# Two-sequence 64x64 products, a first inverse done whole on VectorE, eight steps scored ahead, and one idle product per step in a delta-rule attention kernel with a mixture of experts

## The chip, the cores and the metric

The kernel runs on one core of a Trainium2 chip. The metric is the device time of one execution in microseconds (us), over runs of the same program. One more execution was recorded by the hardware profiler; all durations below come from that one. PE is TensorE (matmuls), PEld its weight loads, DVE is VectorE, ACT is ScalarE, POOL is GpSimd, SP is the engine that issues most transfers. L12 is line 12 of the kernel before.

## The reference

Attention with the delta rule over 4 sequences, 8 heads, 768 tokens, head size 48; its output is reshaped to 3072 tokens of 384 and goes through 8 experts, one per token.

```python
k_n = k / (np.linalg.norm(k, axis=-1, keepdims=True) + 1e-06)
for t in range(S):
    kt, vt, bt = (k_n[:, :, t], v[:, :, t], beta[:, :, t, None])
    y[:, :, t] = np.einsum('bhd,bhde->bhe', q[:, :, t], state)
    v_old = np.einsum('bhde,bhd->bhe', state, kt)
    state = state + bt[:, :, :, None] * np.einsum('bhd,bhe->bhde', kt, vt - v_old)
...
expert_idx = np.argmax(x @ w_gate, axis=1)
h = np.maximum(x_sorted[lo:hi] @ w1[e], 0.0)
y_sorted[lo:hi] = h @ w2[e]
return (gate_w[:, None] * y).astype(np.float32)
```

## The kernel before

The 768 tokens are cut into 24 blocks of 32, one per **step** of the loop at L697. The 128 partitions hold 4 sequences of 32 tokens. Four consecutive steps are a **group**; there are 6 groups. A block is solved with the inverse of a 32x32 triangular matrix per sequence and head, so that a step needs only a few products:

- `by_state` (L453) multiplies keys with the state and gives `R` on top of an identity product of the scaled values (L439); ACT copies it out (L464).
- `logits` (L558, and every fourth step L605 for the ranks) is the router's share for the step before. The instructions in L473 come after ACT has copied the logits (L562).
- The **block product** L473 multiplies the inverse `ub` with `R`: 8 heads times 4 sequences in 32x32 tiles, one per sequence. ACT copies the result to `Z` (L479).
- `by_state` again for the queries (L453 into `pq`), then the state's update (L492), which ACT copies to `states` in two halves (L500).
- The outputs of the step before are turned (L538, copied by L543), then the **masked product** L511 multiplies the masked query-key scores `qk` with `Z`, again 32 products in 32x32 tiles, and ACT copies it to `xg` (L521).
- `score` (L230 in the first `FRONT` = 6 steps, L242 later) makes the key-key and query-key products of a later step. `keep_scores` (L260) masks both on DVE. When a group has its fourth score, `invert` is put on the list `behind`.

The order is written out by hand: each engine works strictly through its own list, in the order of the calls. The inverse is a Python generator; `fill(us)` sends its instructions to DVE in portions, priced with a built-in estimate, 4.0 after each step's products and 2.8 before its `keep_scores`. At the first step of a group, whatever is left of that group's inverse is sent first (L699). When two inverses are on the list, `fill` alternates between them.

The first group's inverse is built in a short form: two 16x16 halves at once on DVE (`K` = 2), and the corner by two products per step on PE (`across`, L384 and L398, with an addition on DVE, L406). These run as `chore`s inside steps 0 to 3. Later groups are inverted whole: 30 pairs of a product (L350) and an addition (L355).

After six scores PE runs ten idle products of 128x512 (`heat`, L431), and one in each step that has nothing left to score. Steps 0, 5 and 8 score one extra step (`EXTRA`). The loads of a step's keys and queries are issued `LEAD` + 2 = 12 steps ahead on SP's queue.

After the loop come the rest of the routing, 24 idle products, and the experts (L775 on), which the change does not touch.

Of the kernel before, what the change touches and what calls it, by code (L numbers as in the profile page):

```python
# [13 lines left out]
FP32 = mybir.dt.float32  # L14
# [26 lines left out]
FRONT = 6  # L41
EXTRA = (0, 5, 8)
LG = DM
RK = LG + E
LEAD = 10
# [4 lines left out]
def _f32_consts():  # L50

    p = np.arange(128)[:, None]
    j = np.arange(128)[None, :]
    rev = np.broadcast_to(E - np.arange(E), (128, E))
    base = np.broadcast_to(np.arange(E) * LIST, (128, E))
    more = np.arange(E)[:, None] * LIST + CAP + np.arange(MAXR)[None, :] * 128  # L60
    more = np.broadcast_to(more.reshape(1, -1), (128, E * MAXR))
    t, w = p % C, j[:, :C]
    own = t // (C // 2) == w // (C // 2)
    kk = 1.0 * (t == w) - (t < w)
    k0 = 1.0 * (t == w) - ((t < w) & own) - (t // (C // 2) > w // (C // 2))
    return np.concatenate(
        [kk, k0, -1.0 * (t < w), rev, base, more, p < j, np.ones((128, 128))], axis=1
    ).astype(np.float32)
# [3 lines left out]
def kernel(  # L72
# [23 lines left out]
    nc.scalar.dma_start(out=cf[:, 0 : 3 * C], in_=src[:, 0 : 3 * C])  # L96
# [4 lines left out]
    def part(w):  # L101
# [4 lines left out]
    mask_g, mask_0, mask_q, rev, base, further, upper, ones = (  # L106
        part(w) for w in (C, C, C, E, E, E * MAXR, 128, 128)
# [51 lines left out]
    warm = persist.tile([128, 512], FP32, name="warm")  # L159
    fdt = persist.tile([128, GS * H, C], FP32, name="fdt")  # L160
# [5 lines left out]
    behind, later, soon, chores = deque(), deque(), deque(), deque()  # L166
    scored, front = [0], [None]
# [3 lines left out]

    def fill(us):


        while us > 0 and behind:
            n = next(behind[0], None)
            if n is None:
                behind.popleft()
                continue
            us -= (0.09 if len(behind) > 1 else 0.165) + 0.00104 * n  # L180
            if len(behind) > 1:
                behind[0], behind[1] = behind[1], behind[0]

    def chore():
        if chores:
            chores.popleft()()
# [62 lines left out]
    def keep_scores(c, pa):  # L249
        if pa is None:  # L250
            return
        g, s = divmod(c, GS)
        if s == 0:
            gts[g] = block.tile([128, GS * H, C], FP32, name="gt", bufs=3)
        qks[c] = stage.tile([128, H, C], FP32, name="qk", bufs=LEAD + 2)
        for out, part, mask in (
            (gts[g][:, H * s : H * s + H, :], pa[:, :, :, 0], mask_g if g else mask_0),
            (qks[c][:], pa[:, :, :, 1], mask_q),
        ):
            nc.vector.tensor_tensor(  # L260
                out=out.rearrange("q (p e) w -> q p e w", e=2), in0=part,
                in1=mask.unsqueeze(1).unsqueeze(1).to_broadcast([128, NP, 2, C]), op=OP.mult,
            )
        if s == GS - 1:
            behind.append(invert(g))

    def invert(g):

        gt = gts[g]
        K = 1 if g else 2
        W = C // K
        ut = block.tile([128, C * C + C], FP32, name="ut")
        full = ut[:, 0 : C * C].rearrange("p (j i) -> p j i", i=C)
        ud = ut[:].rearrange("p (k n) -> p k n", k=K)[:, :, 0 : W * C].rearrange(
            "p k (j i) -> p k j i", i=C
        )
# [12 lines left out]
        if K > 1:  # L291
            nc.vector.memset(full[:, 0:W, W:C], 0.0)
# [38 lines left out]
        w2 = wt[:].rearrange("p (k i) -> p k i", k=K)  # L331

        parts = [(0, W, W)] if K > 1 else [(0, W // 2, W // 2), (W // 2, W, W)]

        def scaled(by_row):
            for a, b, n in parts:
                v = ud[:, :, a:b, 0:n]
                w = w2[:, :, 0:n].unsqueeze(2) if by_row else w2[:, :, a:b].unsqueeze(3)
                nc.vector.tensor_tensor(
                    out=v, in0=v, in1=w.to_broadcast([128, K, b - a, n]), op=OP.mult  # L340
                )
                yield K * (b - a) * n
# [3 lines left out]
        for j in range(W - 2, 0, -1):  # L346
            n = W - 1 - j
            tmp = block.tile([128, C * C // 4], FP32, name="tmp", bufs=4)
            tv = tmp[:, 0 : K * j * n].rearrange("p (k w i) -> p k w i", k=K, i=j)
            nc.vector.tensor_tensor(  # L350
                out=tv, in0=ud[:, :, j + 1 : W, j].unsqueeze(3).to_broadcast([128, K, n, j]),
                in1=ud[:, :, j, 0:j].unsqueeze(2).to_broadcast([128, K, n, j]), op=OP.mult,
            )
            yield K * j * n
            nc.vector.tensor_tensor(  # L355
                out=ud[:, :, j + 1 : W, 0:j], in0=ud[:, :, j + 1 : W, 0:j], in1=tv, op=OP.add
            )
            yield K * j * n
        yield from scaled(False)
        ub = block.tile([128, GS * H, C], FP32, name="ub", bufs=3)  # L360
# [5 lines left out]
        if K > 1:  # L366
            nc.vector.transpose(
                out=fdt[:, :, 0:W].rearrange("p s i -> p i s"),
                in_=full[:, :, 0:W].rearrange("p j i -> p i j"),
            )  # L370
            yield 1024
            for s in range(GS):
                chores.append(partial(across, g, s))
        ubs[g] = ub

    def across(g, s):

        gt, ub = gts[g], ubs[g]
        W = C // 2
        po = front[0][:, 1, DM:512]  # L380
        for h in range(H):
            sh = H * s + h
            for b in range(B):
                nc.tensor.matmul(  # L384
                    po[rows_of(b), W * h : W * h + W], lhsT=gt[rows_of(b), sh, :],
                    rhs=ub[rows_of(b), sh, W:C], start=True, stop=True, skip_group_check=True,
                )
        m1 = work.tile([128, H, W], FP32, name="m1")
        nc.scalar.activation(
            out=m1[:].rearrange("p h w -> p (h w)"), in_=po, func=AF.Copy  # L390
        )

        def second():
            po = front[0][:, 1, DM:512]
            for h in range(H):
                sh = H * s + h
                for b in range(B):
                    nc.tensor.matmul(  # L398
                        po[rows_of(b), W * h : W * h + W], lhsT=fdt[rows_of(b), sh, :],
                        rhs=m1[rows_of(b), h, :], start=True, stop=True, skip_group_check=True,  # L400
                    )
            chores.appendleft(partial(added, po))

        def added(po):
            part = ub[:, H * s : H * s + H, W:C]
            nc.vector.tensor_tensor(  # L406
                out=part, in0=part, in1=po.rearrange("p (h w) -> p h w", h=H), op=OP.add
            )

        chores.appendleft(second)  # L410
# [16 lines left out]
    def heat(n=1):  # L427

        pa = psA.tile([128, 512], FP32, name="pa", tag="pa")
        for _ in range(n):  # L430
            nc.tensor.matmul(  # L431
                pa[:], lhsT=ident[:], rhs=warm[:], start=True, stop=True, skip_group_check=True
            )
# [11 lines left out]
    def step(c):  # L445
# [13 lines left out]
        if c == 0:  # L459
            R = vs  # L460
        else:
            by_state(pc[:, 0, :], 0, False)
            R = work.tile([128, H, D], FP32, name="R")
            nc.scalar.activation(  # L464
                out=R[:].rearrange("q h w -> q (h w)"), in_=pc[:, 0, 0:DM], func=AF.Copy
            )
            logits()
        scale_v(c + 1, 0)
        if c == NS - 1:
            turn(c - 1, psA.tile([128, 512], FP32, name="pa", tag="pa"))  # L470
        for h in range(H):
            for b in range(B):
                nc.tensor.matmul(  # L473
                    pc[rows_of(b), 1, D * h : D * h + D], lhsT=ub[rows_of(b), H * s + h, :],
                    rhs=R[rows_of(b), h, :], start=(h == 0), stop=True, skip_group_check=True,
                )
        chore()
# [10 lines left out]
        if c < NS - 1:  # L488
# [17 lines left out]
            chore()  # L506
        else:
            logits()
        for h in range(H):
            for b in range(B):  # L510
                nc.tensor.matmul(  # L511
                    pq[rows_of(b), D * h : D * h + D], lhsT=qk[rows_of(b), h, :],
                    rhs=Z[rows_of(b), h, :],
# [8 lines left out]
        nc.sync.dma_start(out=xs[128 * c : 128 * c + 128, 0:DM], in_=x)  # L522
        return extra
# [145 lines left out]
    nc.gpsimd.memset(warm[:], 0.0)  # L669
    nc.gpsimd.memset(fdt[:], 0.0)  # L670
    nc.gpsimd.memset(states[:], 0.0)
    nc.gpsimd.memset(empty[:], FAR)
    nc.scalar.dma_start(out=cf[:, 3 * C :], in_=src[:, 3 * C :])
# [10 lines left out]
    ahead = [score() for _ in range(GS, FRONT)]  # L684
    heat(10)
    while 0 not in ubs:
        fill(0.1)
    scale_v(0, 0)
    scale_v(0, 1)
    chore()  # L690
    chore()
# [3 lines left out]
    chore()  # L695
    pieces = deque()
    for c in range(NS):  # L697
        if c % GS == 0:
            while c // GS not in ubs:  # L699
                fill(0.1)  # L700
        extra = step(c)
# [3 lines left out]
        chore()  # L705
# [4 lines left out]
        fill(2.8)  # L710
# [209 lines left out]
```

## Time and profile before

| | us |
|---|---|
| median of three runs | 656.67 |
| lowest and highest | 653.3 and 661.57 |
| the profiled execution | 672.18 |
| its span | 670.4 |
| start, until the first block product | 34.1 |
| the 24 steps, until the last output is stored | 279.5 |
| end of routing, idle products, first gathers | 26.9 |
| experts | 319.3 |
| the rest | 10.6 |

The stages are cut by the starts of single instructions: the first block product at 34.11, the last store of `xg` at 313.55, the first transpose of the experts at 340.51. In the steps PE is busy for 221 of 279.5 us, DVE for 169, ACT for 128. A product in fp32 shows as two weight loads and two matmuls in the records, so 32 products of L473 are 64 entries. A row of the timeline gives start, duration, engine, line, operation, output and inputs, and in brackets how long the engine had been idle and what released it.

### The profile page before, as it was taken

The page shows a single profiled execution, that of the slowest core. Times are in us where ns is not written, and L with a number is a line of the kernel's source. Part 1 is how long each engine was busy: PE and PEld are TensorE (multiplying, and loading weights), DVE is VectorE, ACT ScalarE, POOL GpSimd, SP SyncE. Part 2 cuts the span into 40 slices and gives each one's busy share as a digit, 9 for nine tenths or more (in the row PEclk, how much of TensorE's full clock was granted, in tenths as well). Part 3 has the DMA queues.
Part 4 walks back from the last instruction along what each step waited for, and adds up shares of the span by engine and source line. Part 5 has one row for each costly group of instructions (what it writes and reads, how often), then busy time and mean ns, then how long its engine had stood idle before and what let it go on. Part 6 is the DMA issues. An engine that isn't in the chain of part 4 may idle for free. (4 is left out here: it accounts for less than half of the span.)

```text
span 670.4 us, 18338 instructions
## 1 busy us (share of the span) xinstructions
PE 577.2 (86%) x8120; PEld 358.0 (53%) x8121; DVE 238.6 (36%) x773; ACT 169.2 (25%) x441; POOL 105.4 (16%) x111
## 2 busy tenths in 40 slices
PE   4777758847878988887979999999999999999991
PEld 3356646636656765665435555555555545555550
DVE  4825655789967968011111021111102020111100
ACT  0124325434545556552001010101001010101101
POOL 4000000110010101102240131402213140311011
PEclk9967679787989899888989999999999999999996
DMA  9933336655653334211075012423234342310000
GB/s 320 268 103 98 97 96 194 132 144 136 186 143 105 69 93 92 75 37 26 2 247 197 24 51 106 150 95 121 52 123 132 118 142 106 121 33 36 2 23 12
DMA packets 38882, 72.15 MB, mean 108 GB/s; under 512 B 10310, under 2 KB 25078, under 8 KB 38800
## 3 DMA queue, kind: packets, MB, share of 16 engines
q1 hardware_dynamic: 33072, 60.99, 30.7%
q0 software_dynamic: 4608, 9.47, 4.5%
q8 instruction: 64, 1.05, 0.7%
q10 hardware_dynamic: 1120, 0.50, 0.3%
q14 instruction: 18, 0.15, 0.1%
HBM read 62.16 MB, written 10.35 MB: 108 GB/s over the span
## 5 line engine op out<-in xcount | busy, mean ns | idle before, releaser
L790 PE MATMUL phe<-xTe,w1t 128*128 128x448 f32 x384 | 148.5, 547 | 0.0
L806 PE MATMUL pye<-w2t,hT 128*128 128x384 f32 x384 | 125.1, 486 | 0.0
L790 PEld LDWEIGHTS phe<-xTe,w1t 128*128 128x128 f32 x384 | 73.2, 192 | 70.1 <-issue 67.8
L806 PEld LDWEIGHTS pye<-w2t,hT 128*128 128x128 f32 x384 | 73.0, 190 | 51.7 <-issue 3.0
L633 POOL DMA_INDIRECT lists<-ids,ri x24 | 23.5, 979 | 291.7 <-DVE ut L355 140.9
L795 DVE TENSOR_SCALAR hT<-phe 128x448 f32<-128x448 f32 x32 | 20.0, 625 | 127.5 <-PE phe L790 127.5
L770 POOL DMA_INDIRECT out_dram<-y,rows x24 | 24.0, 1002 | 214.5 <-ACT y L815 181.1
L355 DVE TENSOR_TENSOR ut<-ut,tmp 128x58 f32<-128x58 f32 (+9 forms) x164 | 53.0, 323 | 4.8
L350 DVE TENSOR_TENSOR tmp<-ut 128x58 f32<-128x58 f32 (+9 forms) x164 | 52.7, 322 | 5.1
L799 ACT ACTIVATE hT<-phe 128x448 f32<-128x448 f32 x32 | 17.4, 543 | 144.6 <-PE phe L790 144.6
L419 ACT ACTIVATE vs<-vt,normt 128x48 f32<-128x48 f32 x192 | 47.8, 324 | 7.8 <-DVE normt L324 7.8
L473 PE MATMUL pc<-R,ub 32*32 32x48 f32 x1472 | 25.1, 222 | 24.0 <-DVE tmp L350 10.1
L500 ACT ACTIVATE states<-acc 48x768 f32<-48x768 f32 x46 | 37.0, 804 | 32.8 <-PE acc L492 28.7
L431 PE MATMUL pa<-warm,ident 128*128 128x512 f32 x86 | 43.8, 655 | 0.0
L785 DVE COPY xTe<-px 128x448 f32<-128x448 f32 x24 | 14.2, 614 | 80.7 <-PE px L781 80.7
L815 ACT ACTIVATE y<-pye,xin 128x384 f32<-128x384 f32 x16 | 9.3, 580 | 133.2 <-PE pye L806 133.2
L492 PE MATMUL acc<-Z,kt 32*128 32x96 f32 x736 | 33.3, 324 | 3.3 <-issue 3.3
L473 PEld LDWEIGHTS pc<-R,ub 32*32 32x32 f32 x1472 | 21.2, 119 | 26.9 <-issue 19.2
L558 PE MATMUL pc<-wg,xT 128*128 128x8 f32 x144 | 21.3, 268 | 13.9 <-ACT R L464 10.3
L492 PEld LDWEIGHTS acc<-Z,kt 32*128 32x128 f32 x736 | 28.8, 227 | 8.4 <-issue 6.1
L811 DVE TENSOR_SCALAR y<-pye,xin 128x384 f32<-128x384 f32 x8 | 4.9, 618 | 78.0 <-PE pye L806 78.0
L558 PEld LDWEIGHTS pc<-wg,xT 128*128 128x128 f32 x144 | 19.1, 202 | 18.6 <-ACT R L464 13.6
(109 smaller groups left out, 574.0 us busy)
## 6 DMA issues: line engine op xcount, KB each, us to landing
kq<-in_kq_t_dram SPq DMA_DIRECT2D x24, 512.0 KB
w1t<-in_moe_w_dram SPq DMA_DIRECT2D x7, 1536.0 KB
w2t<-in_moe_w_dram SPq DMA_DIRECT2D x7, 1536.0 KB
kt<-in_k_tok_dram SPq DMA_DIRECT2D x24, 256.0 KB
wkq<-in_kq_t_dram SPq DMA_DIRECT2D x30, 192.0 KB
vt<-in_v_tok_dram SPq DMA_DIRECT2D x24, 192.0 KB
xs<-xg SPq DMA_DIRECT2D x24, 192.0 KB
wkq<-in_kq_t_dram SPq DMA_DIRECT2D x6, 256.0 KB
```

The costliest lines, as they stand in the source:

```text
L350: nc.vector.tensor_tensor(out=tv, in0=ud[:, :, j + 1 : W, j].unsqueeze(3).to_broadcast([128, K, n, j]), in1=ud[:, :, j, 0:j].unsqueeze(2). ...
L355: nc.vector.tensor_tensor(out=ud[:, :, j + 1 : W, 0:j], in0=ud[:, :, j + 1 : W, 0:j], in1=tv, op=OP.add)
L419: nc.scalar.activation(out=vss[c][:, h, :], in_=vts[c][:, h, :], func=AF.Copy, scale=norms[g][:, H * s + h : H * s + h + 1],)
L431: nc.tensor.matmul(pa[:], lhsT=ident[:], rhs=warm[:], start=True, stop=True, skip_group_check=True)
L473: nc.tensor.matmul(pc[rows_of(b), 1, D * h : D * h + D], lhsT=ub[rows_of(b), H * s + h, :], rhs=R[rows_of(b), h, :], start=(h == 0), stop= ...
L492: nc.tensor.matmul(acc[:, b, 96 * p : 96 * p + 96], lhsT=kt[rows_of(b), p, :], rhs=Z[rows_of(b), 2 * p : 2 * p + 2, :], start=(c == 0 and ...
L500: nc.scalar.activation(out=states[r, :, :, e], func=AF.Copy, scale=-1.0, in_=acc[r, :, 0:DM].rearrange("q b (p e w) -> q b p e w", p=NP, e ...
L558: nc.tensor.matmul(pt[:, LG : LG + E], lhsT=xT[:, s, :], rhs=wg[:, s, :], start=(s == 0), stop=(s == NK - 1), skip_group_check=True,)
L633: nc.gpsimd.indirect_dma_start(out=lists, out_offset=bass.IndirectOffsetOnAxis(ap=ri[:, i : i + 1], axis=0), in_=ids[:, ss[i] : ss[i] + 1] ...
L770: nc.gpsimd.indirect_dma_start(out=out, out_offset=bass.IndirectOffsetOnAxis(ap=index, axis=0), in_=y[0:w, :], in_offset=None, bounds_chec ...
L790: nc.tensor.matmul(ph[:], lhsT=w1t[:, s, f * 128 : f * 128 + 128], rhs=xT[:, s, :], start=(s == 0), stop=(s == NK - 1),)
L806: nc.tensor.matmul(py[:], lhsT=hT[:, f, t * 128 : t * 128 + w], rhs=w2t[:, f, :], start=(f == 0), stop=(f == NF - 1),)
```

## The change

- The inverse is spread on ACT to a tile `ubw` that holds, for each head, 64x64 blocks with two sequences on the diagonal and zeros beside them: `spread_out` copies `ub` twice, scaled by a 0/1 column `own`. The query-key scores are masked to the same form, so `qk` doubles. The block and the masked product then take 16 products each in 64x64 tiles where there were 32 in 32x32 tiles.
- `invert` has no short form any more; `across`, `chore`, the tiles `fdt` and `warm` and their clearing on POOL go.
- `FRONT` is 8, `LEAD` 9, `EXTRA` is step 5 alone. The first `fill(8.0)` runs before scores 4 and 5 are masked; 6 idle products follow score 5, 11 follow score 7.
- `fill` takes the two inverses together only while the older is not due in the next group; before `keep_scores` it sends 3.4 instead of 2.8 in the first four steps.
- Each step from 1 on has one idle product of 128x256 (`heat(1, pc[:, 1, 0:256])`) between the logits and the block product. Idle products multiply the identity with itself.

```diff
-FRONT = 6
-EXTRA = (0, 5, 8)
+FRONT = 8
+EXTRA = (5,)
-LEAD = 10
+LEAD = 9
...
     def fill(us):
         while us > 0 and behind:
-            n = next(behind[0], None)
-            if n is None:
-                behind.popleft()
-                continue
-            us -= (0.09 if len(behind) > 1 else 0.165) + 0.00104 * n
-            if len(behind) > 1:
-                behind[0], behind[1] = behind[1], behind[0]
+            two = len(behind) > 1 and GS * behind[0][0] - now[0] > GS
+            for g, work_ in list(behind)[: 1 + two]:
+                n = next(work_, None)
+                if n is None:
+                    behind.remove((g, work_))
+                else:
+                    us -= (0.09 if two else 0.165) + 0.00104 * n
...
-        qks[c] = stage.tile([128, H, C], FP32, name="qk", bufs=LEAD + 2)
+        qks[c] = stage.tile([128, NP, 2, 2, C], FP32, name="qk", bufs=LEAD + 1)
...
+    def spread_out(steps=(0, GS)):
+        g, ub = spread[0]
+        if g not in ubs:
+            ubs[g] = block.tile([128, GS * H, 2, C], FP32, name="ubw")
+        a, b = (H * s for s in steps)
+        for k in range(2):
+            nc.scalar.activation(
+                out=ubs[g][:, a:b, k], in_=ub[:, a:b], func=AF.Copy, scale=own[:, k : k + 1]
+            )
+        if steps[1] == GS:
+            spread.popleft()
...
             logits()
+            heat(1, pc[:, 1, 0:256])
         scale_v(c + 1, 0)
...
         for h in range(H):
-            for b in range(B):
+            for r in two_of:
                 nc.tensor.matmul(
-                    pc[rows_of(b), 1, D * h : D * h + D], lhsT=ub[rows_of(b), H * s + h, :],
-                    rhs=R[rows_of(b), h, :], start=(h == 0), stop=True, skip_group_check=True,
-                )
-        chore()
+                    pc[r, 1, D * h : D * h + D],
+                    lhsT=ub[r, H * s + h].rearrange("q k w -> q (k w)"),
+                    rhs=R[r, h, :], start=(h == 0), stop=True, skip_group_check=True,
+                )
...
         nc.sync.dma_start(out=xs[128 * c : 128 * c + 128, 0:DM], in_=x)
+        if spread and c >= GS * (spread[0][0] - 1):
+            spread_out((1, GS) if c == 0 else (0, GS))
...
-    ahead = [score() for _ in range(GS, FRONT)]
-    heat(10)
-    while 0 not in ubs:
+    for c in range(GS, FRONT, 2):
+        ahead = [score() for _ in range(2)]
+        heat((6, 11)[c // GS - 1 + (c > GS)])
+        if c == GS:
+            fill(8.0)
+            for a in ahead:
+                keep_scores(*a)
+    while not spread:
         fill(0.1)
     scale_v(0, 0)
     scale_v(0, 1)
-    chore()
-    chore()
+    spread_out((0, 1))
...
-        if c % GS == 0:
-            while c // GS not in ubs:
+        if c % GS == 0 and c // GS not in ubs:
+            while not spread:
                 fill(0.1)
+            spread_out()
         extra = step(c)
         fill(4.0)
...
-        fill(2.8)
+        fill(3.4 if c < GS else 2.8)
```

## The prediction

> **What bounds the kernel now.** The chain that ended last covers only the final 4 us, so it says nothing of the part that changes. I read the page's slices first, then the busy time by stage.
>
> ```profile
> PE   4777758847878988887979999999999999999991
> DVE  4825655789967968011111021111102020111100
> PEclk9967679787989899888989999999999999999996
> ...
> 34.10:313.60 279.50, 221.19 (x6531) 168.81 (x6531) 169.02 (x595) 128.15 (x357) 20.11 (x21) 0.85 0.41 108
> 340.50:659.80 319.30, 311.94 (x993) 165.84 (x991) 42.37 (x72) 35.49 (x64) 68.77 (x67) 0.99 0.29 98
> ```
>
> The experts are PE alone at full clock and stay as they are. In the steps no engine is full, and the clock averages 0.85: a latency chain. One undisturbed step, PE then ACT:
>
> ```profile
> 238.27 0.83 PE L558 MATMUL pc<-wg,xT 128*128 128x8 f32 x6 [0.61 <-ACT R L464]
> 239.37 0.88 PE L473 MATMUL pc<-R,ub 32*32 32x48 f32 x64 [0.27 <-ACT lg L562]
> 240.98 1.15 PE L492 MATMUL acc<-Z,kt 32*128 32x96 f32 x32
> 242.53 0.88 PE L511 MATMUL pq<-Z,qk 32*32 32x48 f32 x64
> 243.35 1.13 PE L431 MATMUL pa<-warm,ident 128*128 128x512 f32 x2
> 244.46 0.91 PE L439 MATMUL pc<-vs,ident 128*128 128x384 f32 x2
> 245.30 0.87 PE L453 MATMUL pc<-states,kq 128*32 128x96 f32 x32
> ...
> 242.25 1.63 ACT L500 ACTIVATE states<-acc 48x768 f32<-48x768 f32 x2 [0.55 <-PE acc L492]
> 243.91 0.49 ACT L543 ACTIVATE xT<-pc 128x384 f32<-128x384 f32 x1
> 246.23 0.49 ACT L464 ACTIVATE R<-pc 128x384 f32<-128x384 f32 x1 [1.45 <-PE pc L453]
> ```
>
> The chain runs R, logits, block product, Z, L492, states, xT, L439, L453, next R: 237.73 to 246.23, **8.5 us**. L511 lies beside the states, but it, the idle product and L439 follow one another closely: it has 0.2 us of slack. The 24 steps cost more than 24 times 8.5 (204), and three kinds of row say why:
>
> ```profile
> 98.41 1.50 PE L473 MATMUL pc<-R,ub 32*32 32x48 f32 x64 [7.28 <-DVE ub L362]
> 153.93 1.50 PE L473 MATMUL pc<-R,ub 32*32 32x48 f32 x64 [10.08 <-DVE tmp L350]
> 189.51 0.47 PE L492 MATMUL acc<-Z,kt 32*128 32x96 f32 x5 [1.73 <-issue]
> ```
>
> PE waits 7 and 10 us at steps 4 and 8 for an inverse; it halts in the middle of a row with nothing to wait for (16 such gaps, about 17 us); and the same row of L473 takes 1.50 us at half clock, 0.88 at full.
>
> [...] The trace has stretches of 1.0 and 0.5 only, and low ones follow the gaps above. [...] Here L558, with 8 columns to stream, takes (0.83 - 0.26 for the last) / 5 = 114 ns a matmul. [...] From L439's last start (about 245.2) to L453 there are only about 0.1 us. [...] The halts sit mostly at multiples of 256 PE entries apart[...].
>
> **The change, part by part.**
>
> *Start: +14.5.* DVE begins the first inverse at 13.8; doubled `qk` masking adds 0.4. Whole, the inverse takes 4 transposes 2.1, the norm chain 3.7, scaling 1.1, 60 dependent operations at the later groups' medians by size (19.9 together) plus 34 ns between them (2.0), scaling 0.9, transposes 1.8: 31.5. Masking scores 4 and 5 now stands inside it: 2 x 1.0. It ends at 47.7. Two spreads of 256 elements on ACT (0.5 each, from the 0.32 of a 48-element copy with a column scale plus the slope to 0.49 at 384 without) give 48.6 for the first block product, against 34.1. SP moves two key loads ahead of the wide ones and POOL drops two clearings (1.5 us); both have at least 10 us to spare under the inverse.
>
> *Step 0, to R of step 1: -5.* Before 15.1 us. The corner products (3.6), an extra score (1.1) and part of two halts (3.4) go. The later spread of 24 heads (2 x 0.9) lies under L242, L439 and L453. About 10: R(1) at 58.6, **9.4 behind**.
>
> *One step: +0.8, to 9.3.* The idle product waits for the logits' copy, as L473 did, and L473 queues behind it, so ACT's Z and all after it wait. L439, two matmuls of 384 columns, holds PE 0.85; less 2 x 128 columns at 0.83 ns this leaves **0.64** for 256. It could be 0.45 (two streams of 213 ns, nothing else), or 1.1 at half clock. The block product is 16 sets of four at (0.88 - 0.20) / 16 = 42.5 ns, of which the stream of 48 columns is 40. In 64x64 tiles there are 16 sets of two: the stream is the same, so halving the products saves no stream time. But the load has 64 columns: [...] I take 58: 1.1 us, **+0.22**. No row shows this tile; bounds are 42.5 (load hidden, +0) and 96 (load and stream in series, +0.9). A gain would need a stream shorter than its columns. The masked product grows alike and uses up its slack of 0.2.
>
> *Steps 1 to 3: -16.6.* Before, R(1) to R(4) took 40.6, and 7.0 of waiting for the inverse followed. The corner work and its waits go. DVE's list is now 9.4, 9.1 and 8.2 us between maskings, counted by operation, against PE's 9.3: they run level, 28 us; the group's spread of 1024 elements, 2 x 1.1 on ACT ahead of R(4), costs 2.0; 1 for the clock. 31: **7.2 ahead**.
>
> *Steps 4 to 7: -7.5.* Before 55.5, the wait at step 8 included. After: 4 x 9.3, one routing step +1.45 (L605 and its copy), one extra score 1.1, and a border: DVE's list for a group with its four maskings, and the spread, take 41.8 us from R to R where PE takes 38.6, so R(8) comes about 3.0 late. With halts 3.4 (before 4.5; PE's entries in a step go from 534 to 410, 128 fewer in the two products, 4 more idle) and 2 for the clock: 48. **14.7 ahead**.
>
> *Steps 8 to 23: +10.5.* Before 154.6 for 15 steps: 15 x 8.5, routing 5.8, extra 1.1, halts 7.8, so 12.5 is lost to the clock. After: 15 x 9.3 = 139.5, routing 5.8, borders at 12, 16 and 20 of 3.1, 2.2 and 1.0 (maskings end), halts 6.0, clock 6.6: the idle product raises activity in the emptiest stretch, but each border makes a new hole. 164.2; +0.9 for the last step. **4.2 ahead** at the end. Later stages are not touched.
>
> That sum is against the profiled execution, 672.18, which stands 15.5 above the median. Only halts and clock are irregular enough to hold that; before has 41 of these (17 + 24), after by my terms 21. Scaled by (41 - 15.5) / 41, after gives back 8 where before gives back 15.5. The lead of 4.2 becomes 3 behind: **660 us**.
>
> **The rivals.**
>
> *Loads in series (slower).* If a 64-column load does not lie under the other tile's stream, the period is 96 ns, not 58. The first product adds 0.6 us on the chain, the second 0.6 as well, its slack being used: 1.2 x 23 = 28, so 688. For it: L492, with 128-column loads, takes 112 ns though its stream is 80. Against it: 112 is the load alone, so there the two overlap. It decides above 71 ns: (71 - 58) x 32 x 23 = 9.6 us brings 2% over the median.
>
> *The clock is not held (slower).* Borders of 2 to 3 us are longer than the 0.6 to 2 us halts that now bring half clock. If the loss stays at before's 24 instead of my 9.6, that is 14 more, scaled 9; idle products at half clock (0.4 more, in some 8 steps) add 3: 672. It decides from about 10 more than I took. Against it: the starts of these borders are the only holes left.
>
> *The clock holds and the loads hide (faster).* 0.22 off 22 steps is 4.8, the last clock losses (9.6 x 0.6) 6, and an idle product of 0.45 another 4: 645. For it: from 235 to 268 the clock stays full without any idle product on the chain. Against it: then there was little to win there, and 0.45 a step is paid all the same.
>
> *The spread hides at the borders.* Were DVE early, ACT would spread after `xg` and cost 1.0 each: 655. The lists say otherwise at steps 4, 8 and 12.
>
> **How the numbers follow.** 2% of the median is 13 us, about what a measurement of this kernel can tell: 643.5 to 669.8. Central case 0.53, range 649 to 671 (idle product 0.45 to 0.8, start +-3, clock +-6), a tenth of it above 669.8; spread hidden 0.08; clock and loads better 0.14, over half of it below 643.5; clock not held 0.14, two thirds of it above; loads in series 0.11. Faster 0.08, slower 0.26, same 0.66. Both sides are in reach, so the range goes from 645 to 678.
>
> **What would show it.** First block product near 48.6; R(1) near 58.6; steps of 9.3 where the clock is full; the row of the block product at 1.1 us with 32 entries; the idle product to the block product 0.64 apart; ACT's spread directly ahead of R at steps 4, 8, 12, with DVE's last transpose as releaser; fewer PE halts, and low clock mainly after borders. It would be wrong if the 64x64 row is 0.9 or above 1.4, if the clock in the steps rises above 0.95 or stays at 0.85, or if DVE's list makes R late in the middle of a group.

## The result and the profile after

The kernel after takes **687.88 us** (median of four runs, 681.55 to 695.62), the kernel before 657.69 beside it: a ratio of **1.043** (95% interval 1.032 to 1.054). It is slower; 660 was forecast. Runs that took over 1.5% more than the fastest of their kernel, the profiled one of after among them (695.62, with a span of 693.9 and a mean clock of 0.905), are left out of all ratios and times at half clock below.

The slices of the page after, 17.3 us each:

```profile
PE   3839989798789899898908999999999999999991
PEclk9968889979997878779966999999999999999996
DMA  9804447846743323101282002233434243310000
```

One digit of PE stands out, the 0 at about 355 us. In the same slice the clock is at 6 and DMA at 8; the kernel before has a 9 for PE there. Here is after cut by stage, at the first block product, the last store of `xg` and the experts' first transpose. The columns are the length, the busy time (and count of instructions) of PE, PEld, DVE, ACT and POOL, then the clock, the DMA share and GB/s:

```profile
48.98:321.20 272.22, 240.84 (x4593) 187.70 (x4593) 176.73 (x592) 139.37 (x370) 20.32 (x21) 0.85 0.42 109
321.20:365.20 44.00, 25.23 (x68) 11.66 (x66) 4.34 (x31) 1.28 (x7) 8.78 (x9) 0.80 0.48 154
365.20:683.00 317.80, 312.10 (x992) 165.89 (x992) 42.27 (x72) 35.49 (x64) 68.87 (x68) 0.98 0.25 79
```

The last store stands at 321.2 where it was at 313.55: 7.7 behind. The second stage, which stands behind the edited loop, takes 44.0 us where it took 27: **17 us more**, the larger part of the 23.5 by which the spans differ. The timeline there, SP's issues (start, duration of the issue) and POOL's first gathers:

```profile
340.57 0.39 SPq L133 DMA_DIRECT2D w1t<-in_moe_w_dram  x1
341.01 0.48 SPq L134 DMA_DIRECT2D w2t<-in_moe_w_dram  x1
341.54 3.17 SPq L133 DMA_DIRECT2D w1t<-in_moe_w_dram  x1
344.75 1.69 SPq L134 DMA_DIRECT2D w2t<-in_moe_w_dram  x1
346.48 5.77 SPq L717 DMA_DIRECT2D rows<-lists  x1
352.30 4.02 SPq L721 DMA_DIRECT2D rowh<-lists  x1
361.98 1.04 POOL L741 DMA_INDIRECT xin<-xs,rows  x1 [23.57 <-DMA rowh<-lists]
365.19 0.66 PE L760 MATMUL px<-ident,xin 128*128 128x128 f32 x2 [16.82 <-issue]
```

Four loads of 1.5 MB, the weights of experts 1 and 2, stand ahead of `rows` and `rowh`, two small loads that tell POOL which tokens to gather. POOL stands idle for 23.6 us until they land, and PE for 16.8 us. The same view of the kernel before:

```profile
332.58 0.39 SPq L738 DMA_DIRECT2D rows<-lists  x1
...
336.50 1.04 POOL L762 DMA_INDIRECT xin<-xs,rows  x1 [6.17 <-DMA rows<-lists]
340.51 0.27 PE L781 MATMUL px<-ident,xin 128*128 128x128 f32 x1
340.75 0.39 SPq L132 DMA_DIRECT2D w1t<-in_moe_w_dram  x1
```

The small loads go first and the weights come at 340.75, when the last of the 24 idle products, which read `warm`, has ended. In the source the weights' calls come first in both kernels, so SP's list does not follow the order of the calls here, though that was said of all engines above. What ordered it is not recorded. SP's own waits (us in total, times, longest) show what held the weights, in the kernel before and in after:

```profile
SPq L132 <- PE pa L431: 7.0, 1, 7.0
...
SPq L133 <- DMA lists<-ids,ri: 10.1, 4, 3.6
```

In the kernel before they waited 7.0 us for the last idle product; in after they waited only for the transfers into `lists`, as `rows` has to do anyway. `rows`, issued at 346.48 behind the weights, landed 14.7 us later, where in the kernel before POOL began its gather 3.9 us after the issue.

In the loop itself, here is the timeline of after at the start of step 4, and in step 5 at full clock:

```profile
89.59 2.19 ACT L377 ACTIVATE ubw<-ub,cf 128x1024 f32<-128x1024 f32 x2 [1.54 <-DVE ub L364]
91.69 0.47 ACT L438 ACTIVATE R<-pc 128x384 f32<-128x384 f32 x1
...
105.44 0.70 PE L403 MATMUL pc<-ident 128*128 128x256 f32 x2 [0.27 <-ACT lg L539]
106.07 1.14 PE L448 MATMUL pc<-R,ubw 64*64 64x48 f32 x32
```

At step 4 ACT waits for the inverse, spreads it for 2.19 us, and only then copies R. In step 5 the idle product begins 0.63 ahead of the block product, which takes 1.14.

### The profile page after: what moved, and what is told of

Same layout as the page of the kernel before. It is cut to its first block, busy times and chain, and to the rows that moved or that the text cites. A ratio compares the mean times of both kernels' runs of the same rounds, so it can differ in the third digit from the quotient of the medians.

```text
span 693.9 us, 14515 instructions
## 1 busy us (share of the span) xinstructions
PE 603.7 (87%) x6196; PEld 379.4 (55%) x6197; DVE 261.4 (38%) x809; ACT 180.3 (26%) x451; POOL 104.2 (15%) x109
## 5 line engine op out<-in xcount | busy, mean ns | idle before, releaser
L357 DVE TENSOR_TENSOR ut<-ut,tmp 128x30 f32<-128x30 f32 (+9 forms) x180 | 59.8, 332 | 6.0
L352 DVE TENSOR_TENSOR tmp<-ut 128x30 f32<-128x30 f32 (+9 forms) x180 | 59.4, 330 | 5.9
L403 PE MATMUL pa<-ident 128*128 128x512 f32 x100 | 49.3, 640 | 0.0
L448 PEld LDWEIGHTS pc<-R,ubw 64*64 64x64 f32 x736 | 32.2, 177 | 9.7 <-issue 9.7
L467 PE MATMUL acc<-Z,kt 32*128 32x96 f32 x736 | 35.6, 347 | 0.6 <-ACT Z L454 0.6
L448 PE MATMUL pc<-R,ubw 64*64 64x48 f32 x736 | 35.6, 264 | 0.0
L760 PE MATMUL px<-ident,xin 128*128 128x128 f32 (+1 forms) x96 | 18.9, 303 | 18.9 <-issue 16.8
L467 PEld LDWEIGHTS acc<-Z,kt 32*128 32x128 f32 x736 | 31.4, 251 | 6.0 <-issue 4.2
```

The source lines that it names most:

```text
L352: nc.vector.tensor_tensor(out=tv, in0=full[:, j + 1 : C, j].unsqueeze(2).to_broadcast([128, n, j]), in1=full[:, j, 0:j].unsqueeze(1).to_br ...
L357: nc.vector.tensor_tensor(out=full[:, j + 1 : C, 0:j], in0=full[:, j + 1 : C, 0:j], in1=tv, op=OP.add)
L403: nc.tensor.matmul(out, lhsT=ident[:], rhs=ident[:].unsqueeze(1).to_broadcast([128, out.shape[1] // 128, 128]), start=True, stop=True, ski ...
L448: nc.tensor.matmul(pc[r, 1, D * h : D * h + D], lhsT=ub[r, H * s + h].rearrange("q k w -> q (k w)"), rhs=R[r, h, :], start=(h == 0), stop= ...
L467: nc.tensor.matmul(acc[:, b, 96 * p : 96 * p + 96], lhsT=kt[rows_of(b), p, :], rhs=Z[rows_of(b), 2 * p : 2 * p + 2, :], start=(c == 0 and ...
```

## The experiments

My theory: the order on SP's queue costs some 15 us after the loop; in the loop, idle product and 64x64 tiles each cost what the chain shows, and the clock does not pay it back. Each kernel was compared with runs of the kernel before on its own chip (medians of 667, 659, 672 and 667 us), so only ratios are set side by side. A point is 0.01 of the ratio, some 6.7 us.

| kernel | ratio to before | 95% interval |
|---|---|---|
| after | 1.043 | 1.032 to 1.054 |
| lists first | 1.022 | 1.011 to 1.032 |
| lists first, no idle product | 1.002 | 0.998 to 1.006 |
| lists first, 32x32 tiles | 0.994 | 0.990 to 0.998 |
| lists first, neither | 0.973 | 0.962 to 0.984 |
| before, idle products on `ident` | 1.029 | 1.021 to 1.038 |
| neither, masked product 64x64 | 0.965 | 0.956 to 0.973 |
| neither, block product 64x64 | 1.011 | 1.001 to 1.020 |
| block product 32x32 on the spread inverse | 0.986 | 0.979 to 0.993 |
| neither, old order of `fill` | 0.974 | 0.966 to 0.982 |
| neither, six scores ahead | 0.986 | 0.974 to 0.998 |
| masked 64x64, idle product ahead of the logits | 0.972 | 0.962 to 0.982 |
| the same, in a bank of its own | 0.961 | 0.953 to 0.969 |

**The queue.** First the edit to after, then the one to before.

```diff
-    for e in range(1, 3):
-        weights[e] = load_w(moe_w1[e], moe_w2[e], wnext)
     rows = plan.tile(...)
...
+    for e in range(1, 3):
+        weights[e] = load_w(moe_w1[e], moe_w2[e], wnext)
```

> The changed kernel with the loads of the lists (rows, rowh) issued ahead of the weights of experts 1 and 2. My theory: in the changed kernel these 6 MB of weights stand ahead of two small loads, so that the first gathers come about 17 us late; the loop itself is about 8 us longer. Then this kernel takes about 671 us (688 - 17), the experts begin some 27 us after the last store of xg instead of 44, and it stands 1.02 to the kernel before. Rival: the late start of the experts comes from the idle products or the halved clock, not from the queue; then the time stays within 4 us of 688. Second rival: the weights are then late themselves and the experts wait for them; then 680.

```diff
-    warm = persist.tile([128, 512], FP32, name="warm")
...
-                pa[:], lhsT=ident[:], rhs=warm[:], ...
+                pa[:], lhsT=ident[:], rhs=ident[:].unsqueeze(1).to_broadcast([128, 4, 128]), ...
```

> The kernel before with one edit: its idle products multiply the identity with itself, as the changed kernel's do, and the tile warm and its clearing are gone. Theory: the weights of experts 1 and 2 no longer wait for the last idle product (whose operand lay where they go), so they are issued ahead of rows and rowh, and the first gathers come some 15 us late: ratio 1.02 to 1.025 to the kernel before, 14 us from the end of the idle products to the experts' first transposes instead of none. Rival: the queue order in the changed kernel has another cause (the larger tiles of the loop, freed late); then the ratio is 1.00 within 0.005.

With the lists first the ratio falls by 2.1 points, 14 us of 667 (the two intervals just meet). Its timeline has the small loads ahead, and the experts begin 2.7 us after the last idle product:

```profile
328.93 0.39 SPq L715 DMA_DIRECT2D rows<-lists  x1
...
330.13 0.57 SPq L133 DMA_DIRECT2D w1t<-in_moe_w_dram  x1
333.60 1.04 POOL L741 DMA_INDIRECT xin<-xs,rows  x1 [6.73 <-issue]
340.24 0.30 PE L760 MATMUL px<-ident,xin 128*128 128x128 f32 x1 [2.66 <-issue]
```

The kernel before with nothing but other operands for its idle products loses 2.9 points (2.1 to 3.8), and its timeline shows the order of after:

```profile
322.04 0.39 SPq L132 DMA_DIRECT2D w1t<-in_moe_w_dram  x1
...
327.56 5.78 SPq L737 DMA_DIRECT2D rows<-lists  x1
...
343.35 1.04 POOL L761 DMA_INDIRECT xin<-xs,rows  x1 [23.76 <-issue]
346.53 0.66 PE L780 MATMUL px<-ident,xin 128*128 128x128 f32 x2 [14.73 <-issue]
```

So it is shown: removing `warm` let the weights be issued before the idle products are done, ahead of the lists. The stage after the loop was touched after all, by the operand of its idle products. The second rival, weights that come late in turn, fell: the experts took 329.0 us to the end against 329.9 in the kernel before. SP's wait of 7.0 us for the last idle product, listed in the kernel before and not in the edited one, shows the tie; that it came from the tile's place in memory is the likely reason, but only the tile's removal was tried.

**Idle product and tiles, each alone and both.** "No idle product" takes one line from the kernel with the lists first:

```diff
-            heat(1, pc[:, 1, 0:256])
```

> As the one with the lists first, but without the idle product of 128x256 in each step. Theory: the idle product does not hold the clock and only lengthens the chain by 0.63 us in each of 23 steps: 14 us less than with it, about 657. Rival A: without it PE's activity falls further, the clock in the steps drops by 0.02 to 0.04 and the gain is given back: 667 to 675. Rival B: the idle product fills a time in which PE would wait anyway: within 3 us.

For "32x32 tiles" both products and their masks are written as in the kernel before, and `spread_out` goes:

```diff
-            for r in two_of:
-                nc.tensor.matmul(
-                    pc[r, 1, D * h : D * h + D],
-                    lhsT=ub[r, H * s + h].rearrange("q k w -> q (k w)"), rhs=R[r, h, :], ...
+            for b in range(B):
+                nc.tensor.matmul(
+                    pc[rows_of(b), 1, D * h : D * h + D], lhsT=ub[rows_of(b), H * s + h, :],
+                    rhs=R[rows_of(b), h, :], ...
```

> As the one with the lists first, but block and masked product again as 32 products in 32x32 tiles, without the spread on ACT and with plain masks; the idle product per step stays. Theory: 0.25 us per step on the chain for the block product, as much again where the masked product has no slack, and 2.2 us for the spread at steps 4, 8, 12 and 16: together 12 to 18 us less, about 655. Rival: 64x64 tiles cost nothing on the chain (the clock and the list on DVE set it), 3 us at most; or PE then halts more often, since it has 128 more entries per step: within 5 us of the one with 64x64 tiles.

"Neither" makes both edits.

> As the one with the lists first, without the idle product and with 32x32 tiles: what remains of the change is the whole first inverse, eight scores ahead and the new order of fill. Theory: both costs add: about 643, faster than the kernel before (657) by 2%, with steps of 8.5 us. Rival: the halts and the halved clock come back as in the kernel before and the late start (15 us more) is not earned again: 655 to 665.

The four make a square. The idle product costs 2.0 points with 64x64 tiles and 2.1 with 32x32 (13 and 14 us; its 0.63 in 23 steps is 14.5). The tiles cost 2.7 and 2.9. The costs add, and without both the rest of the change gains 2.7 points. The shortest steps after the first agree: from copy of R to copy of R 9.39 us with both, 8.76 without the idle product, 9.13 with 32x32 tiles, 8.51 with neither. Two copies of R by ACT in the timeline with both:

```profile
273.72 0.49 ACT L438 ACTIVATE R<-pc 128x384 f32<-128x384 f32 x1
283.11 0.49 ACT L438 ACTIVATE R<-pc 128x384 f32<-128x384 f32 x1 [1.45 <-PE pc L427]
```

and with neither:

```profile
251.38 0.49 ACT L410 ACTIVATE R<-pc 128x384 f32<-128x384 f32 x1 [1.78 <-PE pc L399]
259.89 0.49 ACT L410 ACTIVATE R<-pc 128x384 f32<-128x384 f32 x1 [1.45 <-PE pc L399]
```

The idle product does not earn its cost through the clock. Time at half clock in a whole run is worked out as 2 x (1 - mean clock) x span and averaged over the runs of each kernel: 89 us before, 93 with both, 104 without the idle product, 74 with 32x32 tiles, 69 with neither. With 64x64 tiles the idle product takes 12 us off the time at half clock; with 32x32 tiles it adds 5.

**The two products apart.** Both start from "neither": one has only the masked product and its doubled mask in 64x64 tiles, the other only the block product, with the spread.

> The kernel with neither the idle product nor 64x64 tiles, in which only the masked product goes back to 64x64 tiles, with its doubled mask on DVE (0.973 to the kernel before without it). Both together cost 19 us. Theory: block product and spread carry most of it; the masked product costs what DVE takes longer for the masks, in steps 1 to 7, 4 to 6 us: 0.98. Rival: DVE's doubled masks in the steps that wait for DVE, and the masked product's used-up slack, are the larger part: 0.990 or more.

> The counterpart: only the block product in 64x64 tiles, with the spread on ACT, masks plain. Theory: 0.25 us in 22 steps (5.5), the spread at steps 4, 8, 12, 16 and 20 (2.2 each, about 9), 1 us at the start: some 14 us more than without, 0.994. Rival: the spread hides and only the 0.25 per step stays: 0.982.

Both expectations were wrong. The masked product in 64x64 tiles costs nothing that can be seen: with it the ratio is 0.965 where it was 0.973, and where the block product has 64x64 tiles too it is 1.002 with it and 1.011 without. Both differences lie within the intervals. Its step still takes 8.51: it lies beside the states' copy. The block product with its spread costs 3.7 points, 25 us. The next kernel has the spread, and reads it in 32x32 tiles:

```diff
-            for r in two_of:
-                nc.tensor.matmul(pc[r, ...], lhsT=ub[r, H * s + h].rearrange("q k w -> q (k w)"), ...)
+            for b in range(B):
+                nc.tensor.matmul(pc[rows_of(b), ...], lhsT=ub[rows_of(b), H * s + h, b % 2, :], ...)
```

> The kernel without the idle product and with the lists first (64x64 tiles in both products, 1.002 to the kernel before), in which the block product alone is 32 products of 32x32 again but still reads the spread inverse, so that the spread on ACT stays and only the tile changes. With neither spread nor 64x64 block product it is 0.965. Theory: half of the 25 us between the two are the tile (0.25 us on the chain in 22 steps, and the halved clock that follows, since the stretch around R then has less matmul work per microsecond), half the spread (1 us at the start, 2.2 at four or five borders): 0.980. Rival A: the tile is nearly all of it: 0.970. Rival B: the spread is nearly all: 0.995 or more.

At 0.986 it stands between 0.965 and 1.002: some 2.1 points, 14 us, are the spread and 1.6, 11 us, the tile, each to about a point. How the spread costs more than its 2.2 us a border is seen at step 4. The timeline of this kernel:

```profile
85.50 2.19 ACT L377 ACTIVATE ubw<-ub,cf 128x1024 f32<-128x1024 f32 x2 [1.55 <-DVE ub L364]
87.59 0.47 ACT L438 ACTIVATE R<-pc 128x384 f32<-128x384 f32 x1
```

and of the one with only the masked product in 64x64 tiles, which has no spread:

```profile
83.70 0.49 ACT L425 ACTIVATE R<-pc 128x384 f32<-128x384 f32 x1 [1.61 <-PE pc L414]
84.51 0.59 DVE L364 STREAM_TRANSPOSE ub<-ut 128x256 f32<-128x256 f32 x1
85.35 0.88 PE L434 MATMUL pc<-R,ub 32*32 32x48 f32 x64 [0.27 <-ACT lg L522]
```

Without the spread the inverse's last transpose ends 1.4 us after the copy of R has begun, and PE has its weights in time. With it, ACT has to have the whole inverse before it copies R: the inverse is due 2.19 + (85.35 - 83.70) = 3.8 us earlier, and ACT waits 1.55, 3.52, 3.80 and 1.18 us for it at steps 4, 8, 12 and 16. The first and the last are no more than the 1.61 for which R waits for PE without a spread; at steps 8 and 12 some 2 us each come on top of the spread.

The tile's 11 us are more than 22 times 0.25. Here is the kernel with only the block product in 64x64 tiles, cut on the grid of 3.41 us at which its clock changes (columns as in the stages above):

```profile
261.69:265.10 3.41, 2.02 (x50) 1.72 (x44) 0.00 (x0) 2.47 (x7) 0.01 (x1) 1.00 0.39 139
265.10:268.51 3.41, 3.41 (x73) 3.04 (x70) 0.00 (x0) 1.39 (x5) 0.00 (x0) 0.50 0.16 34
268.51:271.92 3.41, 3.41 (x80) 1.76 (x75) 0.00 (x0) 2.48 (x4) 0.00 (x0) 1.00 0.33 106
271.92:275.33 3.41, 2.53 (x65) 2.19 (x66) 0.74 (x5) 1.51 (x6) 0.00 (x0) 1.00 0.18 62
275.33:278.74 3.41, 3.41 (x72) 3.04 (x72) 0.24 (x2) 1.43 (x6) 0.00 (x0) 0.50 0.00 0
```

A stretch of 3.41 us that holds R's copy, the logits and the block product is followed by one at half clock. In the kernel with only the masked product in 64x64 tiles the same kind of stretch was followed by full clock:

```profile
238.70:242.10 3.40, 2.50 (x106) 2.25 (x102) 0.00 (x0) 2.23 (x9) 0.47 (x1) 1.00 0.25 88
242.10:245.50 3.40, 3.40 (x75) 2.60 (x69) 0.00 (x0) 2.70 (x7) 0.00 (x0) 1.00 0.32 89
```

Half clock followed where PE was busy for 2.02 and 2.53 us, and full clock where it was busy for 2.50, so PE's busy share in the profile does not tell the two apart. Pairs of 64x64 products start every 58 ns in step 5 of after, and stream 48 columns each; the sets of 32x32 tiles stream as many every 42.5 ns. So there is less streaming per busy time, by an estimate 40 ns of 58 against 40 of 42.5, at the rate of the count below.

A count over all fourteen profiles fits this. It takes the 912 windows at full clock between 50 and 330 us that lie on such a grid, and adds up in each the time in which columns stream, at some 0.83 ns a column (512 columns of an idle product start every 0.43 us), streams that overlap counted once. The best single limit on streaming time, 1.27 us of the 3.41, tells the windows followed by half clock from the others with 24 errors; the best limit on busy time, 2.37 us, makes 78. No run was made to test it, so this is a fit, not a shown cause. Over whole runs the halved time is 118 us with the block product in 64x64 tiles and 59 with the masked product.

**The rest of the change.**

```diff
-            two = len(behind) > 1 and GS * behind[0][0] - now[0] > GS
+            two = len(behind) > 1
...
-        fill(3.4 if c < GS else 2.8)
+        fill(2.8)
```

> The kernel with neither the idle product nor 64x64 tiles, with the order of DVE's work as before the change: fill alternates between two inverses whenever there are two, and sends 2.8 before the masks in all steps. Theory: of the 18 us by which that kernel beats the one before, the end of the waits of 7 and 10 us at steps 4 and 8 is the most, and these waits came from the alternation: with it R waits again at step 8 and 8 to 12 us are lost: 0.988. Rival: eight scores ahead suffice, and the alternation costs nothing: 0.973 to 0.977.

At 0.974 the new order of `fill` brings nothing that can be seen, and the theory fell. The next kernel has `FRONT` 6, `LEAD` 10, `EXTRA` (0, 5, 8) and ten idle products, as before, with the whole first inverse.

> The kernel with neither the idle product nor 64x64 tiles (0.973), with six scores ahead, ten idle products and extra scores in steps 0, 5 and 8 as before the change; the first inverse stays whole on VectorE. Theory: the second group's inverse starts late, since its last scores come in steps 0 and 1: R waits again at step 4 by some 5 us: 0.982. Rival: it is the whole first inverse, with no corner products in steps 0 to 3, that brings the gain: 0.973.

The 0.986 fits the theory, though its interval and that of "neither" overlap. In its timeline PE's wait for the inverse is back at step 4, and again at step 8 (7.26):

```profile
88.34 1.50 PE L419 MATMUL pc<-R,ub 32*32 32x48 f32 x64 [6.43 <-DVE ub L349]
```

So about half of the 18 us that "neither" gains seems to come from eight scores ahead. What is left goes with the whole first inverse, which was not tried alone.

**An idle product where PE waits.** On the kernel with only the masked product in 64x64 tiles:

```diff
             by_state(pc[:, 0, :], 0, False)
+            heat(1, pc[:, 1, 0:256])
```

> The kernel with only the masked product in 64x64 tiles (0.9646), and the idle product of 128x256 not between the logits and the block product but ahead of the logits, where PE waits 0.6 us for ACT's copy of R. Theory: the halved clock comes from the windows that hold this stretch; filled with matmul work at no cost on the chain, the clock in the steps rises from 0.95 to 0.98 or more and the time falls by up to 6 us: 0.955 to 0.96. Rival: the idle product is longer than the wait (0.63 against 0.61) and what little it adds is lost; the clock stays: 0.965 to 0.972.

Its timeline, PE and ACT in step 19:

```profile
243.16 0.70 PE L390 MATMUL pc<-ident 128*128 128x256 f32 x2
243.89 0.49 ACT L426 ACTIVATE R<-pc 128x384 f32<-128x384 f32 x1 [1.68 <-PE pc L390]
```

The copy of R waits for the idle product, which writes another bank of the same tile. Steps are 9.11 instead of 8.51, and 0.972 falls on the rival's side, but by another mechanism. So it was put after the copy of R in the program, into the tile of the query product, which is taken at the start of the step:

```diff
+        pq = psQ.tile([128, 512], FP32, name="pq")
...
+            heat(1, pq[:, 0:256])
             logits()
...
-        pq = psQ.tile([128, 512], FP32, name="pq")
```

> The kernel with only the masked product in 64x64 tiles (0.9646), with an idle product of 128x256 in PE's wait for ACT's copy of R, written to the bank of the query product (free by then), and issued so that the copy of R does not wait for it, unlike in the run before (0.972), where it did. Theory: the halved clock follows windows that hold this stretch; with matmul work there at no more than 0.1 us of cost, steps stay at 8.5 to 8.7 us, half clock comes only in steps with routing or less, and the time is 0.955 to 0.962. Rival: the clock does not follow the idle product; 0.965 to 0.970.

The same view of that kernel:

```profile
243.67 0.70 PE L390 MATMUL pq<-ident 128*128 128x256 f32 x2
243.81 0.49 ACT L426 ACTIVATE R<-pc 128x384 f32<-128x384 f32 x1 [1.45 <-PE pc L415]
244.35 0.83 PE L519 MATMUL pc<-wg,xT 128*128 128x8 f32 x6
```

Now it is free, and steps are 8.51 again. But time at half clock over the runs is 55 us with it and 59 without, and 0.961 and 0.965 can't be told apart. Both kernels beat the one before and the one after.

## Why the prediction was wrong

- *Start and step 0* were right: the first block product began at 48.98 (48.6 said), R(1) at 59.07 (58.6).
- *One step* was right: 0.63 for the idle product (0.64), 1.14 for the block product (1.1), steps of 9.39 (9.3) where the clock is full, in the kernel with the lists first. The 58 ns taken for a pair of products were my estimate, near half of L558's 114 ns, and 58 were measured. The rival with loads in series, by the same estimate 57 and a stream of 40, so some 97 ns, fell with this. The masked product, said to use up its slack, costs nothing that can be seen.
- *Steps 1 to 7* were right to a few us: R(4) at 91.69 and R(8) at 138.13, where the terms put them at 89.6 and 137.6. The waits of 7 and 10 us went, the spread stood ahead of R at steps 4, 8, 12 and 16, and PE's halts, taken at 9.4 us from step 4 on, nearly vanished (one of over 0.5 us in the loop, 0.60).
- **"Later stages are not touched"** failed. That step looked at PE, ACT and DVE alone. The `warm` tile was listed among what goes, with POOL's clearing as its only effect; what its lifetime held back on SP's queue was not asked. It is 14 us of time, 2.1 points, over half of the miss of 3.8 points (1.043 against 660 / 656.67).
- **The clock, "6.6" for steps 8 to 23 and a loss cut from 24 to 9.6**, was the other failed term, by its size. From R(8) to R(23) 164.2 us were forecast; the profile of after takes 176.2, and the one with the lists first (670.98 us, the lowest of its four runs) 167.6, although no halt of over 0.5 us is left there. An estimate for the latter: 15 steps of 9.39, 5.8 for routing as in the prediction and some 5 at the borders leave 16 us to the clock. Over whole runs with the lists first, half clock takes 93 us, no less than the 89 of the kernel before. That each border makes a new hole was right: in that profile four of the seven halved stretches between R(4) and R(23), 27 of 38 us, begin within 2 us of the copy of R behind a spread. What the prediction did not have is half clock without a hole: in the profile with only the block product in 64x64 tiles, steps 17 and 21, with neither spread nor routing, take 10.29 us, each with a stretch at half clock. The rival "the clock is not held" gave 672, a ratio of 1.023 to the median shown then; with the queue mended 1.022 was measured, but its parts were not measured apart.
- *The scaling to the median* rested on that term, and fell with it. The kernel before also takes 659 us on one chip and 672 on another, so the 15.5 us between its profile and its median need not be halts and clock.

## What to carry to other kernels

When a tile is taken away, ask which transfers waited for its last reader: here an idle operand kept 6 MB of weights behind two small loads that the next stage needs. Put work on the chain only if what it holds up costs less than what it brings; the same idle product cost 0.6 us a step in one place and nothing in PE's wait. And the clock is judged over many runs, not on one profiled execution: in the four runs of the kernel with the lists first its mean went from 0.921 to 0.944.

## What was not expected of the hardware

- Stretches at half clock came in multiples of 3.41 us, but for the last, which the end of the profile cuts: in the profiles of before and after all changes of the clock lie on one grid of 3.413 us, which starts at another point in each. But stretches with PE busy 2.53 and 2.50 us fell on different sides.
- With 6 MB ahead of it, even the issue of a small load took 5.77 us on SP where it took 0.39 in the kernel before.
- Sixteen products in 64x64 tiles in place of 32 in 32x32 went with fewer halts of PE: gaps of over 0.5 us without a wait summed to 9.1 us in the loop with neither, and to 3.0 with the masked product in 64x64 tiles, in one profile each. In the kernel before, all ten such gaps inside a row begin at PE entries that lie multiples of 256 apart, to within one entry, loads and products counted together.
